# A recurrent attention and a soft mixture of experts on one core: a new written order, slot inputs merged unnormalised, and dummy products late

## The chip, the cores and the metric

The kernel runs on one core of one Trainium2 chip. The time is the device time of one execution in microseconds (us). Before the change it is 118.35 us, the median of 3 runs (118.32 to 118.73). A core has a tensor engine (PE, with its weight loads shown apart as PEld), a vector engine (DVE), a scalar engine (ACT), GpSimd (POOL) and a sync engine (SP), each with a queue of its own that is worked through in order, and 16 DMA engines which all queues share.

## The reference

The reference is a recurrence over 768 steps for 4 batches and 8 heads of width 48, whose output is the input x of a soft mixture of 8 experts with 4 slots each:

```python
for t in range(S):                       # S = 768
    cur = einsum('bhd,bhe->bhde', u*k[t], v[t])
    y[t] = einsum('bhd,bhde->bhe', r[t], state + cur)
    state = w[..., None]*state + einsum('bhd,bhe->bhde', k[t], v[t])
x = y as [3072, 384]
logits = x @ phi                         # [3072, 32]
d = softmax of logits over the 3072 tokens
slot_input = d.T @ x                     # [32, 384], 4 slots for each of 8 experts
slot_out = relu(slot_input[e] @ w1[e]) @ w2[e]      # w1 384x1024, w2 1024x384, per expert e
out = (softmax of logits over the 32 slots) @ slot_out   # [3072, 384]
```

## The kernel before

The 768 steps are cut into 6 chunks c of 128. A chunk is loaded as k, r and v, each in two halves over pairs of batches (`load_rkv`, names L0 to L35), with a cast from fp32 to bf16; the first k alone is loaded as fp32 by SP and ACT (L233). Then come the weights w1 (W0 to W7) and w2 (V0 to V6, Va7, Vb7). All but the first loads are issued by POOL, at most eight in flight, and a w2 load waits until the raw k, r, v that its buffer held have been copied. The bytes come in this order and no other.

The work is a set of named tasks, each put by `P.add` on one engine with what it needs, and the text ORDER writes them out by hand: engines get their instructions in the order of the text. A suffix `/D`, `/A` or `/P` chooses DVE, ACT or POOL, numbers choose buffers. Names read so: letters for the kind, then the chunk, then a half or a pair of batches. The kinds that matter here:

- `qk`, `qr`, `qv`: the raw input copied to a padded tile `rp` (L201 on ACT, L203 on DVE). For chunk 0 of k there are two, `qk00` and `qk01`, one for each half that lands.
- `tk`, `tr`, `tv`: 8 transposes each on PE (L355); `ek`, `er` multiply the result by decay tables on DVE (L365); `ev` copies it. The tables are made by `zt` on DVE and `ze` on ACT, four each.
- `A`: 8 score products in one PSUM pair `pA` (L394); `M`: DVE multiplies the 128x1024 scores by a causal mask (L400). There is one `pA`, so the next `A` waits for the `M` before it. There are four per chunk, 24 in all; M000 is the first and M511 the last.
- `bk`, `bv`: 8 transposes back (L376), copied out by `kn`, `vn`; `pr` and `D`, `ds`, `dv`: the term with u; `s`, `S`: the state (L453 on DVE); `Y`: the output products; `x`: their copy; `X`, `xT`: transposed; `l`, `lg`: logits; `mx`, `sb`, `ex`, `c`, `cT`: softmax over slots.
- The softmax over tokens is done in three groups g of chunks (0 to 2, 3 and 4, 5), with a running maximum: `gm`, `gt`, `gl`, `gr`, `gq` find it, `gd`, `gb`, `gx` spread it, `gs`, `ge` make the weights, `dp` sums weighted x for all 32 slots in PSUM, together with the sum of the weights. `gf`, `gg`, `am` rescale the sums so far and `acc` adds the new ones.

After the last group, `rc` takes the reciprocal of the sums of the weights, and `un0` and `un1` multiply the slot inputs by it and put them into the padded tile `uns`. Then four blocks of 12 products with w1 follow (`h00` to `h11`, 512 columns each, four of them side by side in the array), a ReLU copy each (`hs`), transposes (`ht`, `hT`), 64 products with w2 (`o00` to `o75`, one name per expert, the last expert's split in 5 and 3), and 24 output blocks: `p` is the product with the slot weights, `pg` adds to the first four blocks the 3 late products of the last expert, `oe` scales and copies, `dm` stores one, two or four blocks by SP. `rs` and `rr` make the scale. The sum of the products of the first experts is copied in two halves, `so1a` by ACT and `so1b` by DVE; block 0 is also copied in two halves.

PE gets 7 dummy products at the start (`fill`) and none later.

Of the kernel before, what the change touches and what calls it, by code (L numbers as in the profile page):

```python
# [16 lines left out]
iL18 bv01:0,1 ek11 A001:0,1 iL19 qv1:1/A tr10:1,1 vn01:/D tr11:2 M001 iL20 bk10:3,2 vn00:/A tv10:0,1 er11 iL21
A010:0,2 ds0:/A qk2:0/A tv11:5 dv00:0 kn10:/D s00:4,2,0 M010 bk11:3,0 ev10:/A iL22 S101 iL23 S100 ev11:/A s01:2,0,1
kn11:/D iL24 Y001:4 S111 qr2:1/A Y000:3,0 iL25 S110 A011:0,1 dv01:1 bv10:5,2 er10 tk20:0,0 x000:/A M011 tr20:2,0
vn10:/A iL26 tr21:1 s10:3,5,2 er20 iL27 qv2:1/A ek20 A100:0,0 iL28 tk21:2 S201 iL29 bv11:0,3 M100 pr10:0/P tv20:5,0  # L20
vn11:/A ek21 ev20:/A S200 bk20:0,1 x001:/D iL30 bk21:2,2 kn20:/A pr11:/D s11:5,3,3 iL31 qk3:0/D kn21:/A tv21:4 iL32
S211 D1:0,1 iL33 ev21:/A X00:2,0 S210 Y010:3,1 iL34 er21 Y011:5 ds1:/A qr3:1/A A101:0,2 xT00:/D iL35 bv20:4,0
x011:/D dv10:0 l00:0 bv21:1,1 M101 vn20:/A vn21:/A iW0 lg00:/D Y100:2,2 x010:/A iW1 A110:0,1 x100:/A Y101:5 iW2
M110 X01:4,1 iW3 x101:/A s20:0,1,0 dv11:1 xT01:/D X10:3,0 S300 A111:0,0 xT10:/A l01:2 S301 tk30:5,1 iW4 M111 tk31:4
iW5 l10:0 Y110:1,3 qv3:0/A iW6 lg01:/D A200:0,2 ek31 Y111:3 iW7 x110:/D lg10:/A pr20:0/P M200 tv30:2,1 x111:/A
tr30:4,1 ev30:/A tv31:1 mx0 ek30 tr31:0 qk4:0/A X11:3,1 er30 sb0:0/P bk30:2,0 pr21:/D bk31:5,1 A201:0,1 ev31:/A
kn30:/D D2:4,0 kn31:/D ds2:/A M201 xT11:/A bv30:2,2 dv20:0 bv31:1,3 ex0:0 l11:5 vn30:/D s21:4,3,1 vn31:/A lg11:/D
iV0 er31 c0:2 qr4:1/A A210:0,0 dv21:1 Y201:5 S310 M210 Y200:1,4 cT0:/A pr30:0/P s30:0,4,2 x200:/A S311 x201:/A mx1
A211:0,1 S401 Y210:2,5 S400 tk40:1,0 iV1 x210:/A M211 tk41:3 pr31:/P X20:5,0 qv4:0/A ek40 A300:0,2 Y211:4 ek41
xT20:/A M300 s31:0,2,3 sb1:1/P x211:/A zu D3:1,1 tr40:3,0 ex1:1 S410 tr41:5 iV2 ds3:/A S411 c1:4 tv40:0,0 dv30:0  # L30
er40 qk5:1/A tv41:1 cT1:/D bk40:2,2 er41 bk41:3,0 dv31:1 ev41:/A ev40:/D X21:4,1 l20:5 A301:0,0 kn40:/A xT21:/D
bv40:0,0 M301 iV3 kn41:/A bv41:1,1 pr40:0/P l21:4 Y300:2,6 vn40:/A vn41:/D A310:0,1 lg21:/D qr5:0/A Y301:3 lg20:/D
gm0 s40:1,0,0 M310 pr41:/P x301:/A gt0:4 x300:/A gr00 A311:0,2 S501 X30:5,0 gd0 M311 tk50:3,1 iV4 xT30:/A D4:2,0
tk51:4 ds4:/A S500 gb0:0 dv40:0 l30:5 qv5:1/A ek50 A400:0,0 Y311:2 lg30:/D M400 Y310:1,7 tv50:3,1 x311:/A dv41:1
gx0 tv51:5 ek51 x310:/A tr50:0,1 ev50:/D ev51:/A tr51:2 er50 iV5 X31:1,1 A401:0,2 gs0:/P er51 xT31:/A bv50:4,2 M401  # L35
bv51:3,3 vn50:/A pr50:0/P l31:5 s41:0,2,1 lg31:/A vn51:/D ge0 A410:0,1 Y401:1 S511 M410 dp0:4 iV6 pr51:/P S510
A411:0,2 mx3 Y400:5,0 acc0 M411 Y410:3,1 x401:/A x400:/A D5:2,1 x410:/D A500:0,0 iVa7 ds5:/A mx2 X40:0,0 M500
dv50:0 Y411:4 x411:/A xT40:/D A501:0,1 dv51:1 X41:1,1 M501 l40:5 Y500:3,2 xT41:/A sb2:0/D iVb7 A510:0,2 sb3:1/D
lg40:/A Y501:2 x500:/A M510 ex2:0 l41:4 ex3:1 c2:0 lg41:/D x501:/A A511:0,0 gm1 c3:1 cT2:/A X50:5,0 M511 cT3:/A
gt1:3 Y510:4,3 xT50:/A gr10 Y511:2 mx4 x510:/A gq1 sb4:0/P gl0:0 gd1 x511:/A gb1:1 l50:3 ex4:0 gr20 X51:5,1 gx1  # L40
lg50:/D gf1:/D c4:4 xT51:/D gg1 gs1:/P cT4:/D gl1 l51:2 am1:/D ge1 gr21 lg51:/A gq2 dp1:1 mx5 gd2 sb5:1/D ex5:1
gb2:3 acc1 gs2 c5:5 gx2 ge2 gf2:/D gg2 dp2:4 cT5:/D am2:/P rs:0 acc2 rc un0 un1:/D h01:2 rr h11:1 hs01:/A h10:3
hs11:/D h00:5 hs10:/D hs00:/D ht1:4 gG1:0 hT1:/D gG0:2 gG2:1 ht0:3 gE0:/A gE1:/D gE2:/A hT0:/A o00:5 o10 o20 o30
o40 o50 o60 o70 so1b so1a p0:4 p1:2 p2:0 p3:1 pg0 pg1 o75 oe0a oe0b dm00 oe1 so2 pg2 oe2 pg3 dm01 p4:3 p5:5 oe3
p6:4 oe4 p7:2 p8:0 oe5 oe6 p9:1 dm02 p10:3 oe7 oe8 p11:5 p12:4 oe9 oe10 p13:2 dm04 p14:0 oe11 oe12 p15:1 p16:3 oe14
oe13 p17:4 dm10 p18:5 oe16 oe15 p19:0 p20:2 oe18 oe17 p21:3 dm14 p22:1 oe20 p23:5 oe19 oe22 oe21 dm20 oe23 dm24
# [45 lines left out]
def kernel(  # L92
# [566 lines left out]
    P.add("rc", "DVE", lambda e: O(dve.reciprocal(csr[:], acc[:, nM, :])), deps=[f"acc{nG - 1}"])  # L659
# [157 lines left out]
```

## Time and profile before

| what | us |
|---|---|
| median of 3 runs | 118.35 |
| the profiled execution, its own time | 118.51 |
| span of the profiled execution, first to last instruction | 116.7 |
| busy PE, DVE, ACT, POOL | 97.1, 93.4, 75.9, 66.1 |
| first mask M000 starts, last mask M511 ends | 14.87, 80.75 |
| last group's sums `dp2` end, first w2 product `o00` starts | 87.30, 96.18 |
| first four-block store issued | 104.75 |

Times in the views are counted from the first instruction. A row of the timeline gives start, length, engine, line, operation, output and inputs, and how many instructions were merged in it; a row of the windows gives the busy time of each engine in a stretch, the granted clock of PE, the mean busy share of the 16 DMA engines and the bytes per ns they wrote. A group's row gives the count, the busy time and the mean length in ns. Matmul ends are modelled, so PE's busy share says little on how full it is.

### The profile page before, as it was taken

What the parts mean: (1) busy time and instruction counts of PE and PEld (TensorE: products, weight loads), DVE (VectorE), ACT (ScalarE), POOL (GpSimd) and SP (SyncE); (2) the same over time, 40 slices, a digit from 0 to 9 for tenths busy, and PEclk for the clock granted to TensorE, in tenths of its full rate; (3) what the DMA queues carried; (4) which work ended last, traced back from release to release, by engine and by line L of the source; (5) the groups of instructions that cost most, each with busy time, mean ns of one, the idle gap of its engine ahead of it and who ended that gap; (6) DMA issues with size and microseconds to landing.
All of it is one profiled execution on the core that took longest, in us unless ns stands there. A gap on an engine that the chain in (4) does not pass through costs nothing.

```text
span 116.7 us, 3848 instructions
## 1 busy us (share of the span) xinstructions
PE 97.1 (83%) x1624; PEld 75.0 (64%) x1624; DVE 93.4 (80%) x187; ACT 75.9 (65%) x118; POOL 66.1 (57%) x84
## 2 busy tenths in 40 slices
PE   4829999897999999999979999899889959898000
PEld 0329989686988897889958989677564425442000
DVE  6967899999989999999899999997873650299300
ACT  3877399998996899788977872388551060279000
POOL 6935554999899958999998799951210000000000
PEclk9999999999999999999999999999996799999975
DMA  2999999999999999999999999999999993059994
GB/s 34 299 203 207 205 209 206 208 208 206 205 208 218 220 213 216 217 216 208 219 216 215 212 217 215 208 221 216 217 217 211 211 205 66 0 213 394 415 415 181
DMA packets 8992, 25.06 MB, mean 215 GB/s; under 512 B 1168, under 2 KB 5776, under 8 KB 8976
## 3 DMA queue, kind: packets, MB, share of 16 engines
q0 software_dynamic: 7344, 19.27, 84.8%
q1 hardware_dynamic: 1464, 5.16, 11.6%
q10 hardware_dynamic: 168, 0.40, 1.0%
q8 instruction: 12, 0.20, 0.6%
q14 instruction: 4, 0.03, 0.1%
HBM read 39.38 MB, written 4.72 MB: 378 GB/s over the span
## 4 chain that ended last, share of the span: by engine, by line
PE 45%; DVE 30%; issue 7%; DMA 5%; ACT 4%; POOL 1%; ACTq 1%; DVEq 1%; POOLq 0%
DVE AT L400 11%; PE pG L355 10%; PE pG L376 7%; DMA w_all<-in_k_dram 5%; DVE S L453 5%; PE pA L394 4%; PE pG L682 3%; PE pG L754 2%; PE pG L495 2%; PE pG L709 2%; DVE rT L365 2%; PE pG L475 2%; PE pG L469 2%; DVE kT L365 2%; DVE w_all L773 2%
## 5 line engine op out<-in xcount | busy, mean ns | idle before, releaser
L400 DVE TENSOR_TENSOR AT<-pA,mask 128x1024 bf16<-128x1024 f32 x24 | 29.2, 1217 | 0.7 <-PE pA L394 0.6
L201 ACT COPY rp<-raw 128x1536 bf16<-128x1536 bf16 x14 | 20.7, 1487 | 2.8 <-PE pG L355 2.3
L355 PE MATMUL pG<-ident,rp 128*128 128x128 bf16 x288 | 20.7, 230 | 2.1 <-ACT rp L201 2.1
L424 POOL TENSOR_TENSOR dv<-vn,ds 128x768 bf16<-128x768 bf16 x12 | 17.7, 1482 | 4.8 <-ACT ds L201 3.6
L355 PEld LDWEIGHTS <-rp 128*128 128x128 bf16 x288 | 18.1, 103 | 3.0 <-ACT rp L201 2.4
L407 POOL TENSOR_TENSOR pr<-kT,rT 128x1024 bf16<-128x1024 bf16 x8 | 17.1, 2142 | 0.1
L201 ACT CAST x<-pG 128x384 bf16<-128x384 f32 x20 | 9.3, 490 | 4.7 <-PE pG L477 2.6
L394 PE MATMUL pA<-rT,kT 64*128 64x128 bf16 x192 | 9.8, 218 | 1.2 <-DVE AT L400 1.1
L453 DVE TENSOR_TENSOR S<-pG,W 128x384 bf16<-128x384 f32 x20 | 10.4, 547 | 0.0
L201 ACT COPY vT<-pG 128x1024 bf16<-128x1024 bf16 x10 | 10.0, 1023 | 0.5 <-PE pG L355 0.4
L475 PE MATMUL pG<-vn,AT 128*128 128x48 bf16 x192 | 8.7, 183 | 0.0
L773 DVE TENSOR_SCALAR w_all<-pG,rcs 128x384 f32<-128x384 f32 (+1 forms) x13 | 6.9, 596 | 2.2 <-ACT w_all L771 2.2
L394 PEld LDWEIGHTS <-kT 64*128 64x128 bf16 x192 | 5.9, 94 | 4.2 <-issue 3.0
L365 DVE TENSOR_TENSOR kT<-pG,Tk 128x1024 bf16<-128x1024 bf16 x12 | 8.0, 682 | 0.6 <-ACT Tk L309 0.6
L365 DVE TENSOR_TENSOR rT<-pG,Tr 128x1024 bf16<-128x1024 bf16 x12 | 8.1, 683 | 0.3 <-PE pG L355 0.3
L213 POOL DMA_DIRECT2D raw<-in_r_dram x12 | 6.5, 557 | 2.6 <-DMA raw<-in_k_dram 1.8
L213 POOL DMA_DIRECT2D raw<-in_v_dram x12 | 6.3, 531 | 3.0 <-DMA raw<-in_r_dram 3.0
L477 PE MATMUL pG<-dv,ident 128*128 128x384 bf16 x24 | 7.7, 323 | 0.0
L771 ACT ACTIVATE w_all<-pG,rcs 128x384 f32<-128x384 f32 (+1 forms) x12 | 5.8, 586 | 2.7 <-PE pG L762 2.3
L475 PEld LDWEIGHTS <-AT 128*128 128x128 bf16 x192 | 7.1, 96 | 0.2 <-issue 0.2
L201 ACT COPY xT<-pG 128x768 bf16<-128x768 bf16 x7 | 5.6, 800 | 2.5 <-PE pG L495 2.5
L376 PE MATMUL pG<-ident,kT 128*128 128x128 bf16 x80 | 6.2, 237 | 0.9 <-DVE kT L365 0.9
(134 smaller groups left out, 211.6 us busy)
## 6 DMA issues: line engine op xcount, KB each, us to landing
w_all<-in_moe_w_dram POOLq DMA_DIRECT2D x8, 768.0 KB, 19.4
raw<-in_moe_w_dram POOLq DMA_DIRECT2D x7, 768.0 KB, 26.6
out_dram<-w_all SPq DMA_DIRECT2D x5, 768.0 KB, 5.0
raw<-in_r_dram POOLq DMA_DIRECT2D x12, 192.0 KB, 7.1
raw<-in_v_dram POOLq DMA_DIRECT2D x12, 192.0 KB, 7.2
raw<-in_k_dram POOLq DMA_DIRECT2D x10, 192.0 KB, 7.1
raw<-in_moe_w_dram POOLq DMA_DIRECT2D x1, 480.0 KB, 24.4
w_all<-in_k_dram SPq DMA_DIRECT2D x1, 384.0 KB, 4.4
```

The lines of the kernel that those rows point to most:

```text
L201: O(act.copy(dst, src))
L213: O(pool.dma_start(out=raw_t(x)[:, bb * JJ * D:(bb + 1) * JJ * D], in_=src[c, bb]))
L355: O(pe.transpose(o[:, :, j, :], rp_r[W[rp]][:, jh * JH + j].rearrange("p b d -> p (b d)"), ident[:]))
L365: O(dve.tensor_mul(dst, src, (Tk, Tr)[which][:, None, jh].to_broadcast(BC)))
L376: O(pe.transpose(bank_b(kb)[:, h * C:(h + 1) * C], src[:, bl, h].rearrange("p a x -> p (a x)"), ident[:]))
L394: O(pe.matmul(pA[:, bb, h4 * C:(h4 + 1) * C], kt[s, bl, h].rearrange("p a x -> p (a x)"), rt[s, bl, h].rearrange("p a x -> p (a x)"), star ...
L400: O(dve.tensor_mul(AT_r[W[f"AT{key}"]][:], pA[:].rearrange("p bb (h t) -> p bb h t", t=C), mask[:, None, None, :].to_broadcast([128, 2, H ...
L407: O(op(e).tensor_mul(pr_r[W[f"pr{c}"]][:, bl], kT_r[W[f"kT{c}"]][:, bl].rearrange("p h j x -> p h (j x)"), rT_r[W[f"rT{c}"]][:, bl].rearra ...
L424: O(op(e).tensor_mul(dv_r[W[f"dv{c}{bl}"]][:], vn_r[W[f"vn{c}{bl}"]][:], ds_r[W[f"ds{c}"]][:, bl, :, :, None].to_broadcast([128, H, 2, D])))
L453: O(dve.tensor_mul(S_r[W[new]][:, s], bank(kb[hf])[:, 0:HD].rearrange("p (h b d) -> p h b d", b=2, d=D), W128[:, s, :, None].to_broadcast( ...
L475: O(pe.matmul(o[:, z:z + D], AT_r[W[at]][:, bb, h4, :], vn[:, hf * H2 + h4, bb, :], start=(c == 0 and h4 == 0 and bb == 0), stop=False, sk ...
L773: O(dve.tensor_scalar(out=dst, in0=src, scalar1=rcs[:, i:i + 1], scalar2=None, op0=ALU.mult))
```

## The change

1. ORDER is written anew. Some copies change engine. On PE, the products A000 go ahead of `bk00` and `bk01`; the state of chunk 4 (`bk40` to `s41`, and the S50, S51 copies) comes much later, ahead of the last masks; `gm1` comes after M511.
2. Setup: both halves of the first k are issued by SP, one behind the other, and u by ACT. POOL makes its table and the identity ahead of its first load instead of behind it. On ACT three of the four `ze` now come ahead of `qk01`; `qk00` is on DVE.
3. The last `acc` is split: `un0` and `un1` now add the last group's sums from PSUM to the rescaled ones and write the unnormalised result to `uns`. Only the sums of weights are added apart, on 32 columns. `rc` takes their reciprocal on one partition with 128 columns, a product `rv` with a 1x1 identity turns it into a column per slot, `rw` copies it to `hsc`, and `hs` multiplies by it ahead of the ReLU.
4. 17 dummy products of 512 columns on PE, F0 to F16: two after `gl1`, three after `gb2`, two after `dp2`, four between `o50` and `o60`, six between `o60` and `o70`.
5. `so1` and `oe0` are copied whole, by DVE and by ACT. PE does `p0 pg0 p1 pg1` where it did `p0` to `p3` first.

```diff
+WARM = [("gl1", 2), ("gb2", 3), ("dp2", 2), ("o50", 4), ("o60", 6)]
...
-zt1 zc iL6 zt3 ze1 iL7 zw:0 zt0 qk00:0/A iL8 za ze3 iL9 zb zt2 qk01:/A iL10 zd:/D ze2 tk00:0,0 ze0 tk01:1 qr0:1/D
+zt3 zc iL6 zt2 ze3 iL7 zw:0 zt0 ze2 iL8 qk00:0/D ze0 iL9 za qk01:/A zt1 zd:/D zb ze1 iL10 tk00:0,0 tk01:1 qr0:1/D
...
+X50:0,1 x510:/A gm1 Y511:1 xT50:/A mx4 gt1:3 sb4:0/D x511:/A gl0:5 gr10 gq1 ex4:0 l50:4 X51:2,0 gr20 gd1 lg50:/D
+c4:0 xT51:/D gb1:3 cT4:/A gx1 gl1 gs1:/D F0 gf1:/D ge1 gr21 F1 l51:1 gg1 gq2 dp1:4 am1:/D gd2 lg51:/D mx5 sb5:1/D
+gb2:2 F2 acc1 ex5:1 F3 gx2 gs2 F4 gf2:/D ge2 c5:3 gg2 dp2:0 am2:/D cT5:/A F5 F6 acc2 un1 rs:5 rc un0 h10:1 rv:0 rr
+rw:/D h00:4 h01:2 h11:3 hs11:/D hs10:/A hs00:/A ht1:5 hs01:/A gG1:0 hT1:/D gG2:1 gG0:3 ht0:4 gE2:/A gE1:/D gE0:/A
+hT0:/D o00:2 o10 o20 o30 o40 o50 F7 F8 F9 F10 o60 F11 F12 F13 F14 F15 F16 o70 so1 p0:5 pg0 p1:1 pg1 o75 oe1 so2 oe0
...
-    for bb, eng in enumerate((sp, act)):
-        O(eng.dma_start(out=k0[:, bb * JJ * D:(bb + 1) * JJ * D], in_=k_src[0, bb]))
-    O(sp.dma_start(out=u_r[:, :, 0:D], in_=u[:, None, :].to_broadcast([H, 2, D])))
+    for bb in range(2):
+        O(sp.dma_start(out=k0[:, bb * JJ * D:(bb + 1) * JJ * D], in_=k_src[0, bb]))
+    O(act.dma_start(out=u_r[:, :, 0:D], in_=u[:, None, :].to_broadcast([H, 2, D])))
...
+            for q in range(2):
+                def un(e, q=q):
+                    o = 4 * Spe * q
+                    src = bank(kd)[:, 0:nM * ES].rearrange("p (m s) -> p m s", m=nM)[:, :, o:o + 16]
+                    O(dve.tensor_add(
+                        uns[:, :, q, o:o + 144].rearrange("p m (j x) -> p m j x", x=32 + Spe)[:, :, :, 0:Spe],
+                        acc[:, 0:nM, o:o + 16].rearrange("p m (j x) -> p m j x", j=EG),
+                        src.rearrange("p m (j x) -> p m j x", j=EG)))
+                P.add(f"un{q}", "DVE", un, deps=[f"dp{g}", f"am{g}", "zu"], use=[kd])
...
+    P.add("rc", "DVE", lambda e: O(dve.reciprocal(csr[:], acc[0:1, nM, None, :].to_broadcast([1, EG, ES]))),
+          deps=[f"acc{nG - 1}"])
+    P.add("rv", "PE", lambda e: O(pe.matmul(bank("rvb")[:, 0:1], csr[:].rearrange("p j s -> p (j s)"), ident_f[0:1, 0:1],
+                                            start=True, stop=True)), deps=["rc"], take=[("rvb", "G")])
+    P.add("rw", "ACT|DVE", lambda e: copy(e, hsc[:], bank("rvb")[:, 0:1]), deps=["rv"], use=["rvb"])
...
-                    O(act.activation(out=dst, in_=src, func=AF.Relu))
+                    O(act.activation(out=dst, in_=src, func=AF.Relu, scale=hsc[:]))
...
-                for x, e_, m0 in (("a", "ACT", 0), ("b", "DVE", Dm // 2)):
-                    P.add(f"so1{x}", e_, lambda e, m0=m0: copy(e, so1[:, m0:m0 + Dm // 2], bank(SO)[:, m0:m0 + Dm // 2]),
-                          deps=[prev], use=[SO])
+                P.add("so1", "DVE", lambda e: copy(e, so1, bank(SO)[:, 0:Dm]), deps=[prev], use=[SO])
...
+            P.add(f"F{n}", "PE", lambda e: O(pe.matmul(pA[:, 0, :], ones[:, 0:128], ones[:], start=True, stop=True)),
+                  deps=[after, f"F{n - 1}" if n else None])
```

More of the change, by code (lines that the diff above doesn't have):

```diff
@@ L17 @@
[L17 to L46, printed above, removed]
+zt3 zc iL6 zt2 ze3 iL7 zw:0 zt0 ze2 iL8 qk00:0/D ze0 iL9 za qk01:/A zt1 zd:/D zb ze1 iL10 tk00:0,0 tk01:1 qr0:1/D
@@ new lines @@
+vn41:/A M401 tv50:3,1 gs0:/P c2:1 tv51:5 ev50:/A X31:0,0 dv41:1 er50 A410:0,2 ge0 ev51:/D Y401:3 cT2:/A M410 dp0:2
+iV5 xT31:/A ek51 l31:5 A411:0,1 lg31:/A acc0 pr50:0/P mx3 bv50:1,2 M411 bv51:0,3 vn50:/A Y400:4,0 vn51:/D Y410:5,1
+iV6 x401:/A A500:0,0 x400:/A pr51:/P x410:/D Y411:2 M500 X40:1,1 x411:/A bk40:0,2 xT40:/A bk41:3,0 kn40:/D A501:0,2
+sb3:1/P kn41:/A D5:4,1 M501 iVa7 s40:5,2,0 ds5:/A ex3:1 dv50:0 s41:1,0,1 S501 A510:0,1 S500 c3:3 l40:4 M510 dv51:1
+X41:2,0 cT3:/A Y501:5 lg40:/A xT41:/A Y500:3,2 S511 iVb7 A511:0,2 S510 x500:/A l41:4 M511 x501:/A Y510:2,3 lg41:/A
@@ L47 @@
+p2:0 pg2 dm00 p3:3 pg3 oe2 dm01 p4:4 p5:2 oe3 p6:5 oe4 p7:1 p8:0 oe5 oe6 p9:3 dm02 p10:4 oe7 oe8 p11:2 p12:5 oe9
+oe10 p13:1 dm04 p14:0 oe11 oe12 p15:3 p16:4 oe14 oe13 p17:5 dm10 p18:2 oe16 oe15 p19:0 p20:1 oe18 oe17 p21:4 dm14
+p22:3 oe20 p23:2 oe19 oe22 oe23 dm20 oe21 dm24
 """
@@ L644 @@
                 group(g)
-    csr = sb.tile([128, ES], f32, name="csr")
+    csr = sb.tile([1, EG, ES], f32, name="csr")
+    hsc = sb.tile([128, 1], f32, name="hsc")
     def sums(e):
@@ L755, in f @@
                                 start=True, stop=not first))
-                P.add(f"p{i}", "PE", f, deps=(["so1a", "so1b"] if first else ["so2"]) + [f"p{i - 1}" if i else None] + cts,
+                P.add(f"p{i}", "PE", f, deps=["so1" if first else "so2"] + [f"p{i - 1}" if i else None] + cts,
                       take=[(kb, "G")])
```

84 lines of the change are left out of this document (50 added, 34 removed).

## The prediction

> **What bounds the kernel now.** I read the windows first, cut where the kernel changes its kind of work. Columns: PE, PEld, DVE, ACT, POOL busy, then granted clock, DMA share and GB/s.
>
> ```profile
> 13.00:80.70 67.70, 64.92 (x1285) 56.02 (x1283) 66.28 (x109) 55.31 (x79) 56.44 (x61) 1.00 1.09 213
> 84.00:88.00 4.00, 3.50 (x87) 2.89 (x85) 3.20 (x13) 1.66 (x5) 0.46 (x1) 1.00 1.05 217
> 88.00:92.00 4.00, 3.77 (x47) 1.45 (x47) 1.32 (x5) 0.60 (x1) 0.00 (x0) 0.57 1.03 212
> 96.20:99.70 3.50, 2.76 (x61) 1.69 (x62) 0.36 (x1) 0.31 (x1) 0.00 (x0) 1.00 0.31 59
> 99.70:116.70 17.00, 7.60 (x39) 3.40 (x38) 7.33 (x14) 5.83 (x13) 0.00 (x0) 0.87 0.69 278
> ```
>
> The chunks (13.0 to 80.7) are DVE's: it idles 1.42 us of 67.70. Beside it the DMA engines are full (share over 1) until about 96: the loads have a schedule of their own. The last three w2 loads, in the view of that source line, each with its issue and its time to landing:
>
> ```profile
> L219 POOL DMA_DIRECT2D raw<-in_moe_w_dram x1: 597/597/597, 70.4 to 70.4; - x1
> DMA to landing us min/median/max: 24.8/24.8/24.8
> ...
> L219 POOL DMA_DIRECT2D raw<-in_moe_w_dram x1: 591/591/591, 73.1 to 73.1; - x1
> DMA to landing us min/median/max: 24.4/24.4/24.4
> ...
> L219 POOL DMA_DIRECT2D raw<-in_moe_w_dram x1: 591/591/591, 76.8 to 76.8; - x1
> DMA to landing us min/median/max: 22.1/22.1/22.1
> ```
>
> V6 lands at 95.2, Va7 at 97.5, Vb7 at 98.9. They were issued over 20 us earlier, so an earlier issue brings them no earlier. Between M511 and the stores the timeline carries the argument:
>
> ```profile
> 79.53 1.22 DVE L400 TENSOR_TENSOR AT<-pA,mask 128x1024 bf16<-128x1024 f32 x1
> 86.83 0.47 PE L612 MATMUL pG<-dx,x 128*128 128x32 bf16 x12
> 87.41 0.75 PE L653 MATMUL pG<-one_s,cT 128*128 128x1 bf16 x24
> 87.73 0.35 DVE L659 RECIPROCAL csr<-acc 128x32 f32<-128x32 f32 x1
> 88.38 4.41 PE L682 MATMUL pG<-w_all,uns 128*32 128x512 bf16 x48 [0.23 <-DVE uns L663]
> 92.95 0.62 PE L699 MATMUL pG<-ident,kT 128*128 128x128 bf16 x8 [0.16 <-DVE kT L693]
> 93.50 0.82 PE L722 MATMUL pG<-cT,kT 32*128 32x512 bf16 x3
> 93.61 0.69 DVE L203 COPY rT<-pG 128x1024 bf16<-128x1024 bf16 x1
> 95.10 1.03 ACT L201 COPY rT<-pG 128x1024 bf16<-128x1024 bf16 x1
> 96.18 2.77 PE L709 MATMUL pG<-raw,rT 128*32 128x384 bf16 x61 [1.31 <-ACT rT L201]
> 99.39 0.32 ACT L201 CAST vT<-pG 128x192 bf16<-128x192 f32 x1 [3.25 <-DVE vT L203]
> 102.40 0.55 DVE L203 CAST so<-pG 128x384 bf16<-128x384 f32 x1
> 102.93 5.94 DVE L773 TENSOR_SCALAR w_all<-pG,rcs 128x384 f32<-128x384 f32 x11
> 104.75 0.33 SPq L778 DMA_DIRECT2D out_dram<-w_all  x1
> ```
>
> M511 ends at 80.75, dp2 at 87.30, o00 starts at 96.18 (it waited for ACT's `hT0`), o70 ends at 98.95. The store at 104.75 is the first of four blocks; from it the stores are limited by bytes, so the end follows it by 116.7 − 104.75 = 11.95.
>
> **The start.** Chain of waits, timeline, and the queues' shares in 4 to 5 us and in 5 to 6 us:
>
> ```profile
> 1.37 5.96 DMA w_all<-in_k_dram
> ...
> 8.09 0.72 ACT L309 ACTIVATE Tr<-w_all,padb 128x512 bf16<-128x512 f32 x1
> 8.24 3.59 PE L355 MATMUL pG<-ident,rp 128*128 128x128 bf16 x32 [2.11 <-ACT rp L201]
> 14.87 1.22 DVE L400 TENSOR_TENSOR AT<-pA,mask 128x1024 bf16<-128x1024 f32 x1
> ...
> q0 software_dynamic: 104, 0.15, 83.3%
> q10 hardware_dynamic: 31, 0.10, 25.2%
> ...
> q10 hardware_dynamic: 103, 0.29, 87.3%
> ```
>
> The second key half, on ACT's queue, lands at 7.33, behind POOL's r, which got 83% of 4 to 5 us. Now it follows the first on SP's queue, and POOL's first load comes some 0.6 later, behind two small instructions. I take 6.5 or earlier; the ends are 5.1 (the first half's) and 7.33. Then ACT decides: three exponentials of some 0.7 from 4.4 end at 6.5, the copy at 7.35, and PE starts 0.9 earlier. At 3.59/32 = 0.112 each, 48 transposes (k, r, v) take 5.4 and A000 0.5, since `bk` no longer stands ahead of it: M000 starts at 13.3, not 14.87: −1.55. With the late landing it is −0.65. u, 3 KB, now follows w on ACT's queue; PE needs it in `zw` just ahead of `tk00`. I cost it at nothing, w being as small; a later u would hold PE's whole queue for as long.
>
> On this a page of the Trainium skill speaks against the change: "DMA: Bandwidth & Descriptors", section "Queues, rings and completion order", has the engines take turns between queues. By this page of the Trainium skill two halves in one queue get one turn in two where they had two in three, and 7.33 stays. The trace does not agree in this place (25% against 83%, then 87%). It is the third rival.
>
> **The chunks.** DVE's copies between M000 and M511 that change side, by groups of equal shape:
>
> ```profile
> L203 DVE COPY kn<-pG 128x768 bf16<-128x768 bf16 x5 | 2.7, 548 | 0.2 <-PE pG L376 0.2
> L203 DVE COPY xT<-pG 128x768 bf16<-128x768 bf16 x5 | 2.8, 551 | 0.4 <-PE pG L495 0.4
> L203 DVE COPY rp<-raw 128x1536 bf16<-128x1536 bf16 x3 | 1.8, 592 | 0.0
> L203 DVE COPY vT<-pG 128x1024 bf16<-128x1024 bf16 x2 | 1.4, 681 | 0.0
> L407 DVE TENSOR_TENSOR pr<-kT,rT 128x1024 bf16<-128x1024 bf16 x4 | 2.8, 708 | 0.0
> L203 DVE COPY lg_all<-pG 128x64 f32<-128x64 f32 x8 | 1.6, 216 | 0.1
> L557 DVE TENSOR_REDUCE gm<-lg_all 128x32 f32<-128x256 f32 x1 | 0.6, 601 | 0.1
> L407 POOL TENSOR_TENSOR pr<-kT,rT 128x1024 bf16<-128x1024 bf16 x8 | 17.1, 2142 | 0.1
> ```
>
> Eight kn, vn, x leave and three come: −5 × 0.55 = −2.74; xT −4 × 0.55 = −2.20; rp +4 × 0.59 = +2.37; vT +2 × 0.68 = +1.36; pr +2 × 0.71 = +1.42 (pr01 moves behind M000, pr10 comes from POOL); lg −4 × 0.22 = −0.86; gm1 moves behind M511, −0.60; one cT, one sb leave and one ds comes, about −0.5. Sum −1.75, with seven instructions fewer. Neighbours overlap by some 0.08, so −1.2 is time. ACT takes the copies; it was busy 55 of 67.7 us, so I cost them at nothing, and at 0.55 to 0.8 each where ACT is not free.
>
> Against that stands D5: in the new order PE must do it before s40, s41 and A510, while it waits for pr50 and pr51 on POOL (2.14 each and a DMA issue of 0.6 between: 4.9) after ek51, which now stands two masks ahead of it. DVE has some 4 us of work to cover that, then idles. Ends 0 (all covered) and 4.9 (nothing covered); I take 0.6, nearer the cover counted and the idle that DVE shows in all the chunks (1.42). Behind D5 on PE stand s40, s41 and A510, and DVE waits for these with S501, S500 and M510.
>
> M511 ends 1.55 + 1.2 − 0.6 = 2.15 earlier, at 78.6.
>
> **From M511 to o00.** `gs1` moves from POOL to DVE, ahead of gr21, and F0 to F4 stand on PE ahead of dp2. A product of 512 columns takes (0.82 − 0.38)/2 = 0.22 by the three of L722. Most of the five lie in waits; ends 0 and 5 × 0.22 + 0.4 = 1.5, I take +0.45 (mostly gs1). After dp2, F5, F6 and rs (0.43 + 0.65) keep PE until h10, which starts 1.1 behind dp2, as before; so the shorter merge by itself gains nothing. The reciprocal on 128 columns lies between 0.35 (the row of 32) and four times that, 1.4; I take 1.0. It stands on DVE between un1, which h10 needs, and un0, which h00 needs, so rs and h10 (0.65 + 0.65) cover it; `rv` behind it holds PE for up to 0.5 ahead of h00. The new wait of `hs` for `rw` ends near dp2 + 2.5; behind it on ACT stand hs10, hs00 and hs01 (0.6 each), which end by dp2 + 4.3, while ht1 waits for hs11 after the last h block: nothing. If `rw` came 0.8 later they would be what ht1 waits for.
>
> The h blocks are 12 rows of four side by side. At the clock of 88 to 92 (0.57) they took 4.2; at 0.22 they take 2.6. I expect the dummies to hold the clock: PE is then busy with wide products from dp1 on. ht1 starts at dp2 + 5.1 (before 5.65), and `hT0` takes 0.69 on DVE instead of 1.03 on ACT behind the gE copies: 2.7 to o00, before 3.23. In all dp2 to o00 is 7.8 instead of 8.9. With the +0.45, −0.65. o00 starts at 96.18 − 2.15 − 0.65 = 93.4.
>
> On the clock a second page of the Trainium skill bears, "TensorE: Matmul & The Clock Gate", section "Why this matters for your kernels": it asks for no PE gap over about 3 us. The trace differs: in 84 to 88 PE was busy 3.50 of 4.00 by the profile, with no such gap, and yet the clock fell. By that page of the Trainium skill the dummies would have nothing to prevent. That the clock falls with the dummies too is the second rival.
>
> **From o00 to the stores.** Six experts at some 0.33 each (8 of 61 products in 2.77, less the last one's own length) end at 95.35; F7 to F10 add 0.86, o60 0.33, F11 to F16 1.29: 97.8. Va7 landed at 97.5, so the 2.15 of dummies are almost covered. o70 ends at 98.2, before 98.95: −0.75. Without the DMA they would have been dear.
>
> Then the whole copies. so1 takes 0.55 (as so2 at 102.40) where the two halves went one after the other, from 98.95 to 99.71: −0.2. With p0 pg0 p1 pg1 the first stores come up to 1 us sooner, and Vb7 (98.9) is there in time within 0.1. But the four-block store needs so2, oe3, oe5 and oe7 on DVE (0.53 apart: 5.94/11), and oe3 now waits for pg3, which stands behind p0 to p3, the other pg and o75. That costs back most of what the order on PE gives; I take another −0.1, with 0 and −0.4 as ends. The store is issued at 104.75 − 0.75 − 0.3 = 103.7. The end follows, its bytes being the same.
>
> Sum: 118.51 − 1.05 = 117.46. The profiled execution lies 0.16 above the median, so 117.3.
>
> **Rivals.** (1) D5 holds PE, and DVE with it, longer than 0.6. Then o00 comes too late for Va7 to cover the ten dummies in front of o60 and o70: every us after 93.4 is a us at the end. It is slower than now from 1.65 of idle on; at 2.6, half the cover gone, it gives 119.3. For it: DVE's 1.42 in 67.7 left no room, and the cover rests on two masks. Against it: DVE has also the state copies and kn40 in that place, if PE has done s40 in time. (2) The clock falls all the same: 12 rows at 0.43 instead of 0.22, +2.5: 119.8; with half of the rows 118.5. For it: transposes and narrow products looked busy and did not hold it. (3) The key half lands no earlier: +0.9: 118.2, no change. Above all, gains ahead of o00 beyond 0.3 bring nothing, for Va7 and Vb7 land when they do: the floor is 117.0, and 116.6 if the loads end 0.4 earlier.
>
> **Numbers.** Forecast 0.53, for each of its parts has a row and the DMA takes up errors of 0.3 on its one side; D5 0.23, as the largest cost read from an order and from no row; clock 0.12, the wide products being many; key 0.12. What a measurement can tell from no change is about 0.5% (0.6 us): faster is below 117.75. The forecast, some of (3) and small cases of (1) and (2) make 0.57 faster; the rest of (3) and the middle of (1) 0.15 same; 0.28 slower. The forecast's own range is 116.7 to 117.7; 8 in 10 need 116.6 to 119.4.
>
> **What shows it.** M000 at 13.3 and the second key half by 6.5; M511's end at 78.6 with DVE idle under 2.5 since 13; a granted clock of 1 during h, 2.6 long; o00 at 93.4; no PE gap before o70, or a short one; V6, Va7, Vb7 at 95.2, 97.5, 98.9 again. A landing that moves by a us, or an o00 after 95, would make it wrong.

## The result, and the profile after

The changed kernel takes 123.82 us, the median of 4 runs (123.30 to 125.03), against 118.54 for the kernel before beside it: 1.047 times as long (95% interval 1.037 to 1.057). It was predicted at 117.3 and it is slower. Some executions here are about 2% longer than the others at a lower granted clock; the medians count them, the ratios and intervals leave them out. The profiled execution is the shortest of the four, 123.3 us with a span of 121.4.

The windows after, in stages cut as before (columns: PE, PEld, DVE, ACT, POOL busy, granted clock, DMA share, GB/s):

```profile
13.00:83.40 70.40, 66.04 (x1288) 56.79 (x1285) 68.78 (x100) 54.85 (x87) 57.24 (x62) 1.00 1.08 209
87.00:91.00 4.00, 3.79 (x74) 2.78 (x74) 2.89 (x15) 2.44 (x7) 0.00 (x0) 1.00 1.05 217
91.00:95.00 4.00, 3.64 (x71) 1.82 (x67) 1.37 (x5) 1.92 (x3) 0.00 (x0) 1.00 1.03 211
98.40:103.80 5.40, 5.21 (x70) 2.33 (x72) 0.00 (x0) 0.00 (x0) 0.00 (x0) 1.00 0.09 17
103.80:121.40 17.60, 7.47 (x39) 3.41 (x39) 7.51 (x14) 5.98 (x12) 0.00 (x0) 0.87 0.67 269
```

The clock holds through the h blocks (1.00 where it was 0.57). But when the w2 products begin at 98.4 the DMA engines are nearly idle (17 GB/s): nothing there waits for a load any more. The timeline after, rows as those shown of before (L800 is a dummy, L697 h, L680 `rv`, L708 `hs11`, L724 w2):

```profile
82.17 1.23 DVE L403 TENSOR_TENSOR AT<-pA,mask 128x1024 bf16<-128x1024 f32 x1 [0.33 <-PE pA L397]
...
90.02 0.47 PE L615 MATMUL pG<-dx,x 128*128 128x32 bf16 x12
...
90.75 0.94 DVE L678 RECIPROCAL csr<-acc 1x128 f32<-1x128 f32 x1
91.44 0.83 PE L697 MATMUL pG<-w_all,uns 128*32 128x512 bf16 x12
92.21 0.38 PE L680 MATMUL pG<-ident_f,csr 1*128 1x1 f32 x2
92.51 2.13 PE L697 MATMUL pG<-w_all,uns 128*32 128x512 bf16 x36
94.75 0.75 DVE L708 TENSOR_SCALAR kT<-pG,hsc 128x512 bf16<-128x512 f32 x1 [1.97 <-ACT kT L706]
95.65 0.61 PE L714 MATMUL pG<-ident,kT 128*128 128x128 bf16 x8 [1.01 <-DVE kT L708]
97.66 0.69 DVE L206 COPY rT<-pG 128x1024 bf16<-128x1024 bf16 x1
98.41 2.13 PE L724 MATMUL pG<-raw,rT 128*32 128x384 bf16 x48 [0.85 <-DMA raw<-in_moe_w_dram]
100.70 0.81 PE L800 MATMUL pA<-ones 128*128 128x512 bf16 x3 [0.16 <-issue]
101.44 0.51 PE L724 MATMUL pG<-raw,rT 128*32 128x384 bf16 x8
101.89 1.47 PE L800 MATMUL pA<-ones 128*128 128x512 bf16 x6
103.28 0.50 PE L724 MATMUL pG<-raw,rT 128*32 128x384 bf16 x5
...
109.49 0.33 SPq L789 DMA_DIRECT2D out_dram<-w_all  x1
```

M511 ends at 83.40 (before 80.75), the last sums at 90.49 (87.30), `o00` starts at 98.41 (96.18), o70 ends at 103.78 (98.96), the four-block store goes out at 109.49 (104.75). The end follows by 11.94, as before. The row of 98.41 names a DMA as its releaser. The row of 97.66, DVE's copy `hT0`, fits better: it ended at 98.35. The last w2 loads, first V5, V6 and Va7 (issued at 70.8, 74.7 and 77.8), then Vb7:

```profile
L222 POOL DMA_DIRECT2D raw<-in_moe_w_dram x3: 591/597/599, 70.8 to 77.8; - x3
DMA to landing us min/median/max: 21.2/21.9/22.2
...
L222 POOL DMA_DIRECT2D raw<-in_moe_w_dram x1: 591/591/591, 81.2 to 81.2; - x1
DMA to landing us min/median/max: 19.9/19.9/19.9
```

V6 landed at 96.6, Va7 at 98.9, Vb7 at 101.1. So o60 (101.44) and o70 (103.28) began 4.8 and 4.4 after the loads they need. Of the 4.74 us lost up to the four-block store, 2.65 are there by the end of M511 and 2.59 come between `o00` and o70's end; between M511 and `o00` 0.42 is gained, and behind o70 0.08.

In the chunks two groups of DVE have become longer. These rows answer to the `rp` and `pr` rows shown of before (592 and 708 ns there):

```profile
L206 DVE COPY rp<-raw 128x1536 bf16<-128x1536 bf16 x6 | 5.7, 958 | 0.0
L410 DVE TENSOR_TENSOR pr<-kT,rT 128x1024 bf16<-128x1024 bf16 x4 | 5.2, 1307 | 0.0
```

DVE's work from M000 to M511, each instruction counted at the shortest time of its line and shape, less the overlap of 0.08, fell from 62.3 (104 instructions) to 61.0 (97): −1.3, where −1.2 was predicted. Yet the stretch grew from 65.88 to 67.23. The timeline of GpSimd and DVE says where, in four places:

```profile
13.58 2.67 DVE L206 COPY rp<-raw 128x1536 bf16<-128x1536 bf16 x1
13.69 2.13 POOL L410 TENSOR_TENSOR pr<-kT,rT 128x1024 bf16<-128x1024 bf16 x1
...
24.79 1.54 POOL L427 TENSOR_TENSOR dv<-vn,ds 128x768 bf16<-128x768 bf16 x1
25.07 1.81 DVE L410 TENSOR_TENSOR pr<-kT,rT 128x1024 bf16<-128x1024 bf16 x1
...
40.26 1.55 POOL L427 TENSOR_TENSOR dv<-vn,ds 128x768 bf16<-128x768 bf16 x1
40.30 2.06 DVE L410 TENSOR_TENSOR pr<-kT,rT 128x1024 bf16<-128x1024 bf16 x1
...
43.27 1.47 POOL L427 TENSOR_TENSOR dv<-vn,ds 128x768 bf16<-128x768 bf16 x1 [0.44 <-ACT ds L204]
44.02 0.27 DVE L519 TENSOR_REDUCE mx<-lg_all 128x4 f32<-128x128 f32 x1
```

In the first three places a DVE copy or product whose operands are all in SBUF meets a product on GpSimd, and ends 0.43 to 0.55 after that product. Alone it takes 0.55 or 0.68, so this is what it looks like when DVE waits for GpSimd's product to end and runs then. The three cost 2.1, 1.1 and 1.4 us. Two inside the chunks make 2.5; with −1.3 of work and 0.2 more of other idle time that is +1.4, and +1.35 was measured. DVE work with an operand in PSUM (masks, `ek`, `er`) runs beside the same products at its usual length. So does the reduction `mx` of the fourth place, though it reads and writes SBUF alone: 0.27 here, and 0.26 to 0.29 in all the places of these runs where it met a product. Being in SBUF is thus not enough to be held.

### The profile page after: what moved, and what is told of

Read it like the earlier page. It is cut to its first block, busy times and chain, and to the rows that moved or that the text cites. A ratio compares the mean times of both kernels' runs of the same rounds, so it can differ in the third digit from the quotient of the medians.

```text
span 121.4 us, 3881 instructions
## 1 busy us (share of the span) xinstructions
PE 100.3 (83%) x1640; PEld 76.4 (63%) x1643; DVE 96.2 (79%) x182; ACT 74.3 (61%) x124; POOL 65.4 (54%) x82
## 4 chain that ended last, share of the span: by engine, by line
DMA 38%; PE 17%; DVE 17%; POOL 9%; issue 6%; ACT 4%; POOLq 1%; SPq 1%; DVEq 1%; ACTq 0%
DMA w_all<-in_moe_w_dram 19%; DMA raw<-in_moe_w_dram 14%; DVE AT L403 5%; DMA w_all<-in_k_dram 5%; PE pG L358 5%; PE pG L767 4%; DVE rp L206 4%; PE pG L724 3%; POOL w_all L219 3%; POOL pr L410 2%; POOL dv L427 2%; DVE rT L368 2%; DVE kT L368 2%; ACT rp L204 2%; PE pA L800 2%
## 5 line engine op out<-in xcount | busy, mean ns | idle before, releaser
L358 PE MATMUL pG<-ident,rp 128*128 128x128 bf16 x288 | 21.5, 235 | 4.0 <-ACT rp L204 2.4
L358 PEld LDWEIGHTS <-rp 128*128 128x128 bf16 x288 | 19.1, 106 | 5.2 <-ACT rp L204 2.4
L204 ACT COPY rp<-raw 128x1536 bf16<-128x1536 bf16 x9 | 13.4, 1489 | 0.6 <-PE pG L358 0.6
L782 ACT ACTIVATE w_all<-pG,rcs 128x384 f32<-128x384 f32 x12 | 6.0, 599 | 8.8 <-PE pG L775 8.5
L204 ACT COPY vT<-pG 128x1024 bf16<-128x1024 bf16 x7 | 6.9, 1018 | 5.9 <-PE pG L358 5.7
L204 ACT COPY vn<-pG 128x768 bf16<-128x768 bf16 x10 | 8.0, 806 | 2.7 <-PE pG L379 2.7
L204 ACT COPY xT<-pG 128x768 bf16<-128x768 bf16 x11 | 8.7, 804 | 0.2 <-PE pG L498 0.2
L784 DVE TENSOR_SCALAR w_all<-pG,rcs 128x384 f32<-128x384 f32 x12 | 6.5, 611 | 2.2 <-PE pG L775 2.2
```

Of the source, the lines that this page charges most:

```text
L204: O(act.copy(dst, src))
L358: O(pe.transpose(o[:, :, j, :], rp_r[W[rp]][:, jh * JH + j].rearrange("p b d -> p (b d)"), ident[:]))
L784: O(dve.tensor_scalar(out=dst, in0=src, scalar1=rcs[:, i:i + 1], scalar2=None, op0=ALU.mult))
```

## The experiments

**The first stall put into the kernel before, and taken out of the changed one.**

```diff
 e3, in the kernel before
-pr00:0/D
+pr00:0/P
 e2, in the changed kernel
-qk1:1/D
+qk1:1/A
```

> The kernel before with one product, pr00, moved from DVE to GpSimd. Theory 'DVE waits for GpSimd': qk1 or pr01, which DVE starts while GpSimd is at pr00, grows from 0.55 or 0.68 to over 1.5 us, M000 starts 0.5 to 1.5 later and the end is 0.5 to 1.5 us later, 119 to 120. Rival 'DVE's sum of work sets the end' (the prediction's rule): DVE has 0.68 less to do, the end is 0.3 to 0.6 us earlier, 117.8 to 118.1.

> The changed kernel with one copy, qk1, moved from DVE to ACT, which is idle there. Theory 'DVE waits for GpSimd' (the copy took 2.67 us, of which 2.13 while pr00 ran on GpSimd): M000 starts at 14.1 instead of 16.2, and the end comes 1.5 to 2.1 us earlier, 121.7 to 122.3. Rival 'the copy was late for another reason, or DVE makes it up before M511': end within 0.5 us of the changed kernel.

e3 took 119.32 us, 1.010 (1.006 to 1.015) times the kernel before. It takes a product of 0.7 us off DVE, and yet M000 is 0.75 later and M511 0.85. Its timeline:

```profile
12.55 2.12 POOL L415 TENSOR_TENSOR pr<-kT,rT 128x1024 bf16<-128x1024 bf16 x1 [0.60 <-DVE rT L373]
12.85 2.25 DVE L211 COPY rp<-raw 128x1536 bf16<-128x1536 bf16 x1
```

The copy that took 0.55 to 0.6 takes 2.25. Less work on DVE, by a product on GpSimd, made DVE later.

e2 took 124.59 us, 1.052 (1.044 to 1.059): no gain. M000 came at 14.12, 2.05 earlier, as the stall theory has it, but M011 at 27.83 and the end of M511 at 83.33, both as in the changed kernel. (The longer time has another cause as well: in the profiled execution the granted clock was 0.50 from 98.6 to 102.0, in the w2 products.) The timeline shows the gain turned into a wait:

```profile
14.70 1.47 ACT L212 COPY rp<-raw 128x1536 bf16<-128x1536 bf16 x1
...
16.88 1.29 DVE L376 TENSOR_TENSOR kT<-pG,Tk 128x1024 bf16<-128x1024 bf16 x2 [1.54 <-PE pG L366]
```

ACT does the copy later and in 1.47 us, PE's transposes wait for it, and DVE waits 1.54 for these. The other stalls stayed. So the first stall explains the late M000, but taking it away alone brings M511 no earlier.

**The three products kept apart.**

```diff
 e5, in the changed kernel
-pr00:0/P
+pr00:0/D
-pr10:0/D
+pr10:0/P
-pr11:/D
-M011
+M011 pr11:/D
-dv11:1
-pr20:0/P
+dv11:1 pr20:0/P
 e6: e5, and W0 to W3 issued ahead of pr20
-dv11:1 pr20:0/P
+iW0 iW1 dv11:1 iW2 iW3 pr20:0/P
 e7: e6 without F7 to F16
```

> The changed kernel with its three long products kept apart on DVE and GpSimd: pr00 back on DVE, pr10 back on GpSimd with pr11 behind M011, and dv11 ahead of pr20 on GpSimd, where that engine idled. Theory (DVE waits for GpSimd's running product): the instructions of 2.67, 1.81 and 2.06 us take 0.6 to 0.7; M000 starts at 14.1, and M511 ends at 83.4 - 2.05 - 2.5 + 0.1 = 79 to 79.7; o00 at 94.0 to 94.7. Then the loads decide: if the last w2 part still lands at 101.1, the first block can't end before it, the four-block store goes out at about 105.5 and the time is 119.5 to 120. Rival (the new chunk order itself costs, by PE's and ACT's order): M511 ends after 81.5 and the time stays above 121.5.

> The same, with the issues of W0 to W3 ahead of pr20 on GpSimd. If the low transfer rate at 36 to 42 us is what makes the last w2 loads late, the slices of 151 and 192 GB/s are gone, the last three land at 95.2 to 95.7, 97.5 to 98.0 and 98.9 to 99.4, the four-block store goes out near 104.8 and the time is 118.3 to 118.8. Rival (the loads are late for another cause, or do not decide): landings and time as in the kernel with the products apart alone.

> The same without the ten late dummy products. If the landings cover them, as the prediction had it, the time is within 0.4 us of the kernel with them. If they are still on the path, it is 0.8 to 2.1 faster; by the landings at 97.5 and 98.9 I expect 0.6 to 0.9 faster: 117.5 to 118.

All three missed: 124.41, 124.31 and 123.99 us (ratios 1.050, 1.048 and 1.039). M000 came at 14.3 to 14.4, but M511 ended at 84.3 to 84.5. Other instructions met other products, as these rows of e5's DVE show:

```profile
21.17 2.10 DVE L214 COPY rp<-raw 128x1536 bf16<-128x1536 bf16 x1
...
27.69 2.06 DVE L418 TENSOR_TENSOR pr<-kT,rT 128x1024 bf16<-128x1024 bf16 x1
...
44.54 1.45 DVE L530 TENSOR_TENSOR sd<-lg_all,mx 128x128 f32<-128x128 f32 x1
```

They ran beside dv00 (21.35 to 22.85), dv01 (27.67 to 29.20) and a third `dv` (44.38 to 45.85). The stalls had moved and were as many. pr10 also stood ahead of loads on GpSimd, and the transfer rate fell to 173 to 191 GB/s between 27 and 43 us. W0 to W3 ahead of pr20 (e6) did not cure that: the rate was 165 to 184 from 27.5 to 36.7 us, and the last loads came no earlier (V6 97.97, Vb7 101.68). Whether the rate decides the landings stays open. e7 left out the ten dummies and gained almost nothing; in its profiled execution the clock was 0.63 in the w2 products, which took 4.33 us, and its end is in the table below. These edits of the order moved the stalls and did not remove them, so they can't settle what the stalls cost.

**GpSimd's products made short, everything else left.**

```diff
+    for t in pr_r + dv_r:
+        O(dve.memset(t[:], 0.0))
...
-                O(op(e).tensor_mul(pr_r[W[f"pr{c}"]][:, bl], kT_r[W[f"kT{c}"]][:, bl].rearrange("p h j x -> p h (j x)"),
-                                   rT_r[W[f"rT{c}"]][:, bl].rearrange("p h j x -> p h (j x)")))
+                hs = slice(0, H if e == "DVE" else 1)
+                O(op(e).tensor_mul(pr_r[W[f"pr{c}"]][:, bl, hs], kT_r[W[f"kT{c}"]][:, bl, hs].rearrange("p h j x -> p h (j x)"),
+                                   rT_r[W[f"rT{c}"]][:, bl, hs].rearrange("p h j x -> p h (j x)")))
...
-            O(op(e).tensor_mul(dv_r[W[f"dv{c}{bl}"]][:], vn_r[W[f"vn{c}{bl}"]][:],
-                               ds_r[W[f"ds{c}"]][:, bl, :, :, None].to_broadcast([128, H, 2, D])))
+            O(op(e).tensor_mul(dv_r[W[f"dv{c}{bl}"]][:, 0:1], vn_r[W[f"vn{c}{bl}"]][:, 0:1],
+                               ds_r[W[f"ds{c}"]][:, bl, 0:1, :, None].to_broadcast([128, 1, 2, D])))
```

The same edit was made in the changed kernel (x1) and, as the control, in the kernel before (x2). Both leave out seven heads of eight of what GpSimd multiplies.

> The changed kernel, with GpSimd's products cut to one head of eight (the rest of their output is left out and stays zero; the waits and the order stay). Theory (DVE waits for GpSimd's running products, and that is what makes the chunks late): no DVE product or copy is longer than its fellows by more than 0.3 us; M000 starts at 14.1 to 14.4 and M511 ends at 14.2 + 61.2 of work + 2 to 3 of small losses = 77.5 to 78.5, which is what the prediction had (78.6). Rival (the new order holds DVE by waits of its own, and the stalls only stand where idle time would be): M511 ends after 81.

> The same cut in the kernel before, as the control (the same part of the output is left out). By the theory it loses only its 0.7 us of such stalls: M511 ends at 79.5 to 80.5, later than in the changed kernel with the cut. Rival: M511 moves by 2 us or more here too, as in the changed kernel, and the stalls explain no difference between the two.

The groups of DVE in x1:

```profile
L206 DVE COPY rp<-raw 128x1536 bf16<-128x1536 bf16 x6 | 3.3, 555 | 0.0
L413 DVE TENSOR_TENSOR pr<-kT,rT 128x1024 bf16<-128x1024 bf16 x4 | 2.7, 683 | 0.0
```

The means are back from 958 and 1307 to 555 and 683 ns, M000 starts at 14.59 and M511 ends at 79.33, 4.07 earlier. In the control (119.97 us, 1.001, 0.995 to 1.007), the stretch from M000 to M511 went from 65.88 to 65.40; in the changed kernel from 67.23 to 64.74. With the products short, the changed kernel's chunks are the faster ones by 0.66; with them whole, the slower by 1.35. Both kernels missed the time expected for the end of M511 by 0.7 to 0.8 (79.33 against at most 78.5, and 81.19 in the control against at most 80.5): the memsets lie on DVE ahead of the chunks, and in the control M000 came 0.9 later. x1 still took 120.11 us (1.012, 1.004 to 1.020). In its profiled execution the clock fell to 0.50 in the first w2 products and the ten dummies followed, so o70 ended at 101.13, 3 us after Va7 had landed.

**The ten late dummies.**

```diff
 e1, in the changed kernel: - F7 ... F16
 e4, in the kernel before
+o50 F0 F1 F2 F3 o60 F4 F5 F6 F7 F8 F9 o70
```

> The changed kernel without the ten dummy products behind o50 and o60. Theory 'on the path' (o00 starts at 98.4, V6 and Va7 have landed by 96.6 and 98.9, so nothing hides the ten): o70 and the end come 10 x 0.215 = 2.1 us earlier, 121.7. Rival 'covered by the loads' (what the prediction said): within 0.4 us of the changed kernel, 123.4 to 123.8, with a gap on PE ahead of o60 or o70.

> The kernel before with only the ten late dummies, four behind o50 and six behind o60. Theory 'on the path': +2.1 us, 120.5, since o00 starts at 96.2 and Va7 has landed at 97.5 when o70 could start at 98.5. Rival 'the dummies hold the clock or wait for loads that PE would have waited for': +0.5 or less.

e1 took 122.57 us (1.039, 1.031 to 1.048), e4 123.19 (1.039, 1.030 to 1.048). In e1 o70's end and the store came 2.2 earlier, in e4 2.4 later: the ten are on the path in both orders. But e1's span fell by only 0.8 and e4's rose by 3.8. Both lost 1.4 behind the four-block store, where the end followed by 13.35 and 13.31 in place of 11.95.

**What the 1.4 us are.** The queues' shares of e1 in 108 to 110 us, in the middle of its stores (packets, MB, share):

```profile
q1 hardware_dynamic: 144, 0.76, 96.5%
q8 instruction: 1, 0.02, 3.0%
```

Beside the stores (q1) there is one packet of 16 KB of code (q8). The kernel before has 12 such packets (the row of its page below), the last at 92.8 us; e1, e4 and the changed kernel have 13, and the changed kernel's last came at 105.6, ahead of its first store.

```profile
q8 instruction: 12, 0.20, 0.6%
```

That gave a theory to try both ways: more PE instructions, ten tiny products on PE at 6 us, where it idles (c1); and fewer, the kernel before with the new end (b1) and then with 18 PE instructions less (b3).

```diff
 c1: zw:0 + ten products of one column
 b1, in the kernel before: F0 to F6, the new merge, so1 and oe0 whole, p0 pg0 p1 pg1
 b3: b1 - 7 products of the setup, - 2 of F0 to F6
```

> The kernel before with ten products of one column more on PE at 6.1 us, where PE waits for the first copy: no step moves by them. In the runs so far the time from the four-block store's issue to the end was 11.95 where no 16 KB of code were fetched during the stores, and 13.3 where they were, which was in the kernels with a PE stream of 3275 to 3279 instructions. Theory (the fetch delays the stores that share its DMA engine): the fetch appears after 102 us, the tail grows to 13.3 and the time is 119.5 to 119.9. Rival (the tail has another cause, or the count does not decide): 118.2 to 118.6.

> The kernel before up to the last sums, then the new end: seven dummies around the last group, the merge that leaves out the division, its scale at the ReLU, the copies whole and p0 pg0 p1 pg1; no late ten. M511 ends at 80.7 as before; by the changed kernel's own rows (7.0 to 7.1 from M511 to the last sums with two steps on DVE; 7.9 from there to o00) o00 is at 95.5 to 95.8 and the four-block store at 104.1 to 104.4: 117.6 to 118.0. Rival (the tail's gain is lost to the loads, which land when they do): o70 ends at 98.7 or later and the time is 118.2 to 118.5.

> The kernel before with the new end, five dummies instead of seven and without the seven products at the start: 18 PE instructions fewer than in the kernel with the new end, and as many as the kernel before has. Theory: no code is fetched during the stores, the tail is 11.95 and the time 118.0 to 118.6 instead of 120.3, if the clock holds at the start and in the h blocks (3.2 long, dummies or not; 4.4 if the last five do not hold it). Rival: tail of 13.3, time 119.8 to 120.5.

| kernel | PE and PEld instructions recorded | packets of code | last one | store to end |
|---|---|---|---|---|
| before | 3248 | 12 | 92.8, before the stores | 11.95 |
| changed | 3283 | 13 | 105.6, before the stores | 11.94 |
| e1 | 3264 | 13 | 108.6, in the stores | 13.35 |
| e4 | 3267 | 13 | 108.5, in the stores | 13.31 |
| e7 | 3264 | 13 | 110.6, in the stores | 13.32 |
| c1 | 3268 | 13 | 109.4, in the stores | 13.38 |
| b1 | 3264 | 13 | 106.0, in the stores | 13.39 |
| b3 | 3247 | 12 | 95.9, before the stores | 11.97 |

c1 adds nothing but instructions in an idle place and gets the longer end. (It took 122.33 us, 1.015, 1.004 to 1.026, more than the 119.5 to 119.9 expected; the clock was 0.62 in the w2 products of its profiled execution, so only its end is used.) b1 took 120.32 (1.016, 1.007 to 1.024): its four-block store goes out at 104.63, 0.12 ahead of the kernel before, and the fetch costs more than that. b3 took 117.97. In all five kernels where a packet fell among the stores the end is the longer one, and in none of the others: the price of a fetch is where it falls. SP issued e1's stores at the same pace as before, but the one behind the four-block store took 5.7 us to land in place of 4.2, so the time is lost in the transfers, not on PE or SP. That the packet holds up the stores of one of the 16 DMA engines is the likely way; no run here shows it.

The Trainium skill, "Runtime: NRT & Kernel Launch", section "Instruction fetch mechanics", has the sequencer fetch its code in blocks of 16 KB, 256 instructions, at a mostly hidden cost. The packets' size agrees. Among the stores it was not hidden; what it costs in the chunks no run here shows.

**Dummies, clock and merge.**

```diff
 b4: b3 without its five dummies
 b5, in the kernel before: five dummies, no products in the setup, nothing else
 n1: b3 with the old merge (rc, un0, un1; no rv, rw, hsc)
 k1, in the kernel before: both key halves by SP, u by ACT
```

> The kernel before with the new end and without the seven products at the start, as the one just run, and without its five late dummies. Theory (the dummies hold the clock): the granted clock falls in the h blocks, which take 4.2 to 5.3 instead of 3.2; from the last sums to o00 8.9 to 9.6 instead of 7.9; o70 still waits for Va7, so o70's end moves by 0.3 to 1.0 and the time is 118.3 to 119.0. Rival (the merge is what made it shorter): h 3.2, no change.

> The kernel before with its own merge and end, five dummies (three behind gb2, two behind dp2) and without the seven products at the start. Theory (dummies hold the clock, the new merge by itself gains nothing): h takes 3.2 instead of 4.4, o00 comes 7.7 to 8.0 after the last sums, and the time is within 0.4 us of the kernel with the new end and the same dummies. Rival (the merge gains too): o00 8.3 or more after the last sums and 0.5 us or more slower.

> The kernel before with the new merge and end, five dummies and no products at the start, once more, to be compared with the next one on the same chip. If its gain is the held clock and the store some 0.5 us earlier, and not a chance of one chip: 117.7 to 118.2 again, 0.2 to 0.6 us ahead of the undisturbed runs of the kernel before; if not, within 0.2 us of these.

> The same with the old merge (division ahead of w1, no scale at the ReLU) in place of the new one; hT0 on DVE, the copies whole and p0 pg0 p1 pg1 stay. With the dummies and the old merge, o00 came 7.24 after the last sums, with the dummies and the new merge 7.91. Theory (the new merge costs, its gain was the dummies' alone): o00 comes 6.8 after the last sums, at 94.1; then Va7's landing at 97.5 to 98.1 decides, o70 ends at 98.2 to 98.6 and the time is 117.5 to 118.0, within 0.3 of the other. Rival (the new merge is needed): o00 7.9 or more after the last sums.

> The kernel before with both halves of the first k issued by SP and u by ACT, nothing else. In the runs so far the second half landed at 7.3 to 7.7 in kernels that start like the one before, at 7.6 to 8.1 in kernels that start like the changed one. If the queue decides (one after the other in one queue): 7.8 or later here. If it is GpSimd's setup ahead of its first load: 7.3 to 7.6. What the prediction had: 6.5.

b4 took 120.94 us (1.016, 1.007 to 1.025). The h blocks take 5.7 us, nearly all of it at half clock:

```profile
87.89 1.47 PE L702 MATMUL pG<-w_all,uns 128*32 128x512 bf16 x12
89.29 0.58 PE L685 MATMUL pG<-ident_f,csr 1*128 1x1 f32 x2
89.80 3.79 PE L702 MATMUL pG<-w_all,uns 128*32 128x512 bf16 x36
...
88.00:92.00 4.00, 4.00 (x38) 1.54 (x38) 0.54 (x4) 1.36 (x2) 0.00 (x0) 0.50 1.03 212
```

b5 took 118.52 (0.999, 0.995 to 1.003). Its h blocks, with the old merge, take 2.77 in one piece, and `ht1` follows 0.15 behind them:

```profile
88.44 2.77 PE L691 MATMUL pG<-w_all,uns 128*32 128x512 bf16 x48
91.37 0.62 PE L708 MATMUL pG<-ident,kT 128*128 128x128 bf16 x8 [0.15 <-DVE kT L702]
```

So dummies hold the clock in the h blocks, and they did not need the new merge. All the profiles say so: in the twelve with dummies ahead of the h blocks the clock is 1.00 through them, in the seven without it is 0.50 to 0.65. From the last sums to `o00` it is 8.88 before, 10.46 with the new merge alone, 7.91 with both (b3), 7.24 with dummies alone (b5) and 6.71 in n1, which has `hT0` on DVE too. (The 10.46 holds more time at half clock than the 8.88, so their difference is not the price of the merge.) The new merge costs 1.2 us (b3 against n1): `rv` between the h blocks 0.43, and 0.85 because in its order h11 comes last and `ht1` waits for its copy; that second part belongs to the order that was written for it.

b5's `o00` is 1.6 earlier than before, and yet b5 is no faster: in its profiled execution the clock fell in the w2 products, 0.62 over the 4.39 us that they took (2.77 before), and o70 ended at 99.00 as it did before (98.96). In five of the twelve profiles the fall came there. The dummies moved it, and did not always avoid it.

b3 again took 118.33 (1.001, 0.997 to 1.005), so its first result, 0.984 (0.975 to 0.993), does not stand as a gain. n1 took 117.67, 0.996 (0.992 to 0.9995) of the kernel before: 0.4% faster, only just clear of no change, and one of many versions tried. No other version here stands as faster.

k1 took 118.52 (1.000, 0.998 to 1.003; two runs), with the second key half at 7.48 in its one profile. Kernels that start as before had it at 7.26 to 7.66, those that start like the changed one at 7.57 to 8.07. SP's one queue brings nothing and costs nothing here. Why it is a little later in the changed kernel stays open: GpSimd's setup ahead of its loads, the other change there, was not tried alone.

## Why the prediction was wrong

- **The start** (M000 at 13.3): 16.17. Of the 2.87, 0.8 is the key half, landed at 7.57 and not by 6.5: rival 3, and the one in which the Trainium skill's "DMA: Bandwidth & Descriptors" ("Queues, rings and completion order") was held against the trace. Its result, no earlier landing, is what k1 and the changed kernel show. The share of 25% read in one microsecond was no rate to reckon with. The other 2.05 is the stall of `qk1` beside pr00: e2, without it, had M000 at 14.12.
- **The chunks** (−1.2 of work, +0.6 for D5): the work fell by 1.3. D5's idle is of the size that was taken: DVE idles 0.90 between M411 and M511, before 0.42. What failed, and what made the kernel slower, is the step from work to time: each product and copy that changed sides was priced by its own duration, at "−1.2 is time". The rows used (592 and 708 ns) came from places where GpSimd ran no product. But pr00 moved to GpSimd (2.13), `rp` copies and pr10 moved to DVE, and they met GpSimd's products. That is 2.5 us inside the chunks and 2.05 ahead of M000, and x1 gives 4.07 of it back at M511. The two parts don't simply add: e2 took away the 2.05 alone and M511 came no earlier. The prediction named neither this cost nor a bound for it.
- **M511 to the last sums** (7.0): 7.09. **To `o00`** (7.8): 7.92, with the reciprocal at 0.94 (1.0 taken), the h blocks at 3.20 with `rv` among them (2.6 and 0.5 taken), and a clock of 1.00. The sum was right. "The shorter merge by itself gains nothing" was too kind: it costs 1.2, and the dummies gave 1.6 where the prediction counted the two together. On the clock the trace was the better guide than the Trainium skill's "TensorE: Matmul & The Clock Gate" ("Why this matters for your kernels"): without any gap of 3 us, b4's h blocks ran at 0.50 and b3's, with five dummies ahead of them, at 1.00.
- **The ten dummies** (covered by Va7's landing): the cover hung on `o00` at 93.4, and `o00` came 5.0 later. From `o00` to o70's end it took 2.6 us longer than before, and e1, without the ten, has 2.2 of that back at the store. The prediction said so as its condition; rival 1 had this consequence, from another cause. The loads themselves were taken to land as before (95.2, 97.5, 98.9). They were issued 4.3 to 4.7 later and landed 1.4 to 2.3 later, which cost nothing here only because PE came later still.
- **The whole copies and the new order** (−0.3): from o70's end to the four-block store 5.71, before 5.79: −0.08. That is less than its ends allowed (−0.2 for `so1`, then 0 to −0.4 for the order); `so1` ended 0.67 behind o70 in place of 0.76, and the order gave nothing. **The end** (+11.95): +11.94.

By the prediction's own steps the four-block store was due at 103.7 and it came at 109.49. The difference of 5.8 is 2.87 (start) + 1.95 (chunks) + 0.2 (to `o00`) + 0.57 (`o00` to the end of o70, 4.8 taken) + 0.2 (to the store). So 4.8 of 5.8 came up to M511.

On the stall a page bears that the prediction did not weigh: the Trainium skill, "SBUF — State Buffer", section "SBUF: two separate sides", has VectorE and GpSimd share a pair of SBUF ports which the first takes for its whole instruction, while the other, if it is a VectorE instruction with two SBUF inputs or in a fast mode, fully blocks. The rows above agree: the wait ends with GpSimd's instruction, and neither the instructions with an operand in PSUM nor the reduction `mx`, with its one input, show any. Which copies are in a fast mode no row shows, nor who came first: the copy of 13.58 is recorded 0.11 ahead of the product that it waited for.
